# Attention followed by an MLP on one core: score matmuls of two key slots back to back, 112-wide query tiles, a six-bank tail and new pacing

## The chip, the cores and the metric

The kernel runs on one core of a Trainium2 chip. The metric is the device time of one execution in microseconds (us). Ratios below use runs in the fast state alone. Medians are of all runs of a kernel; a_single and a_fix_r2 each hold one slow run, which is said there. Each experiment ran on one chip together with runs of the kernel before. The changed kernel itself ran only in the first rounds, so a difference in us to it crosses rounds (the medians of the kernel before lay between 497.8 and 500.1 us in them); the ratios to the kernel before are the safer comparison.

AV stands for attention times V, the second product of the attention. The names of the engines are those of the profile: PE is TensorE's matmuls, PEld its weight loads, DVE is VectorE, ACT ScalarE, POOL GpSimd.

## The reference, cut to what matters

```python
# q, k, v: (8, 12, 448, 64) float32, g_q and g_k: (64,)
q_n, k_n = rmsnorm(q, g_q), rmsnorm(k, g_k)
scores = q_n @ k_n.transpose / sqrt(64)
attn   = softmax(scores)
x      = (attn @ v), heads put side by side      # (3584, 768)
h      = x @ w_in                                # (3584, 2048)
g      = h * clip(h + 3, 0, 6) / 6
out    = g @ w_out                               # (3584, 768) float32
```

There are 8 batches of 12 heads. The kernel takes two heads at a time, a pair: 48 pairs, six to a batch. When the six pairs of a batch are done, its MLP can begin.

## The kernel before

The kernel does not issue its operations in source order. It records each with a cost, a wanted time and the resources that it reads and writes. A small list scheduler, the plan, then orders them: each engine takes, of what it takes to be available, the operation with the earliest wanted time. So the order on every engine is fixed when the program is built, by a model of the hardware; at run time each engine works through its list, and semaphores make it wait where the model was too hopeful. PE writes its results to banks of PSUM; the first lines of the cut share these banks out. "Gate" in the cut is the last product of g, a VectorE operation.

```python
S_r = [psum.tile([128, 2, 512], FP32, name=f"S{i}") for i in range(2)]   # 2 tiles of 2 banks
X_ps = psum.tile([128, 2, 512], FP32, name="X")                          # 2 banks
M_r = [psum.tile([128, 512], FP32, name=f"M{i}") for i in range(2)]      # 2 banks

def score(P, t, want):            # one of four key slots of a pair, 112 keys
    # ... [cut]
    def f_s():
        for a in range(2):        # the two heads: rows 0-63 and 64-127 of the array
            r = slice(a * 64, a * 64 + 64)
            em(nc.tensor.matmul(out=ps[:, a, 0:S], lhsT=kT[r, t * TP:t * TP + 128], rhs=qT[r, :], ...))
    def f_e():
        em(nc.scalar.activation(out=eT[:, t], in_=ps[0:TP, :, 0:S], func=EXP, bias=0.0, scale=1.0))

C0 = [0, 128, 256, S - 128]       # four query tiles of 128, the last two overlap
def av(P, t, want):
    # ... [cut]
    for a in range(2):
        for i in range(NQT):
            em(nc.tensor.matmul(out=X_ps[:, a, i * E1:(i + 1) * E1],
                                lhsT=eT[:, t, a, C0[i]:C0[i] + 128], rhs=va[:, a, t, :], ...))

# MLP: 16 h groups of a batch (6 matmuls of 448 columns, relu on ACT, gate on DVE),
#      y groups (2 x 16 matmuls of 384 columns, copy on ACT); banks M0 and M1 in turn
em(nc.scalar.activation(out=ts[:], in_=ps[:, 0:S], func=RELU, bias=half_c[:], scale=1.0 / 6.0))
# ... [cut: loads, normalisation, transposes, output]

T0, DP0, DP = 8.0, 4.0, 8.5       # wanted times: a pair every 4 us, from the second batch on every 8.5 us
...
base = at(P + 1)                  # MLP work of a batch is spread from the start of the next batch on
span = at(P + NPAIR + 1) - base
```

The transposes of q and k go into the score tiles S0 and S1, in turn with the scores.

## Time and profile before

| kernel before | |
|---|---|
| time, median of the first 3 runs | 499.28 us (498.3 to 501.03) |
| PE busy | 461.8 us, 93% of the span |
| ACT, DVE, POOL busy | 59%, 47%, 43% |
| chain that ended last | PE 81% |
| score matmuls, busy | 72.5 us |

A timeline of the kernel before, PE only, shows what a score pair costs (columns: start, duration, instruction; the ends of matmuls overlap the next start):

```profile
200.12 0.36 PE L303 MATMUL S<-qT,kT 64*128 64x448 bf16 x2
200.42 1.47 PE L397 MATMUL M<-w_out_sb,gT 128*128 128x384 bf16 x8
201.73 0.39 PE L342 MATMUL X<-identity,xn 128*128 128x128 bf16 x4
```

Eight w_out matmuls take 1.31 us from their first start to the next instruction's, 163 ns each. The two score matmuls run side by side in the two halves of the array, but the next instruction starts 0.30 us after them, not the 0.19 us that 448 columns take elsewhere (a w_in matmul: 189 ns). And 0.1 us is lost on the way in. Over the whole trace a trip into half-array mode and back costs about 0.2 us, and there are 173 of them. That is the term that the change attacks.

### The profile page before, as it was taken

The page shows a single profiled execution, that of the slowest core. Times are in us where ns is not written, and L with a number is a line of the kernel's source. Part 1 is how long each engine was busy: PE and PEld are TensorE (multiplying, and loading weights), DVE is VectorE, ACT ScalarE, POOL GpSimd, SP SyncE. Part 2 cuts the span into 40 slices and gives each one's busy share as a digit, 9 for nine tenths or more (in the row PEclk, how much of TensorE's full clock was granted, in tenths as well). Part 3 has the DMA queues.
Part 4 walks back from the last instruction along what each step waited for, and adds up shares of the span by engine and source line. Part 5 has one row for each costly group of instructions (what it writes and reads, how often), then busy time and mean ns, then how long its engine had stood idle before and what let it go on. Part 6 is the DMA issues. An engine that isn't in the chain of part 4 may idle for free.

```text
span 497.3 us, 10192 instructions
## 1 busy us (share of the span) xinstructions
PE 461.8 (93%) x4160; PEld 264.9 (53%) x4160; DVE 234.5 (47%) x432; ACT 295.1 (59%) x485; POOL 213.6 (43%) x204
## 2 busy tenths in 40 slices
PE   1688999899998999899999999999999999989996
PEld 0355556456555555565555555555555555545563
DVE  4766576465864255545546254455434233322200
ACT  5566778767775367656666475666657456533311
POOL 4886594598963146536256063545223000000000
PEclk9999899999999999999999999999999999999999
DMA  7999984254422145333233243332110111111122
GB/s 207 254 245 265 243 190 127 75 161 140 136 74 89 34 125 144 96 97 98 87 110 92 70 125 92 101 97 85 55 32 2 33 34 34 34 32 30 34 59 69
DMA packets 44463, 50.99 MB, mean 103 GB/s; under 512 B 3456, under 2 KB 40832, under 8 KB 44416
## 3 DMA queue, kind: packets, MB, share of 16 engines
q1 hardware_dynamic: 39040, 44.05, 31.4%
q0 software_dynamic: 5376, 6.29, 7.2%
q8 instruction: 32, 0.52, 0.4%
q14 instruction: 15, 0.12, 0.1%
HBM read 45.61 MB, written 11.01 MB: 114 GB/s over the span
## 4 chain that ended last, share of the span: by engine, by line
PE 81%; DMA 7%; DVE 3%; ACT 3%; issue 2%; POOL 2%; SPq 1%; POOLq 0%; ACTq 0%; DVEq 0%
PE M L397 30%; PE M L364 26%; PE S L303 9%; PE X L320 9%; DMA qk<-in_k_dram 6%; PE S L283 3%; PE X L342 2%; ACT eT L308 2%; DMA qk<-in_q_dram 1%; DVE gT L375 1%; ACT ts L372 1%; POOL qks L253 1%; DVE xn L335 1%; SPq L201 1%; DVE ssq L227 0%
## 5 line engine op out<-in xcount | busy, mean ns | idle before, releaser
L308 ACT ACTIVATE eT<-S 112x896 bf16<-112x896 f32 x192 | 171.8, 916 | 61.4 <-PE S L303 59.9
L364 PE MATMUL M<-xT,w_in_sb 128*128 128x448 bf16 x768 | 171.0, 354 | 4.1 <-DVE gT L375 3.8
L397 PE MATMUL M<-w_out_sb,gT 128*128 128x384 bf16 x896 | 160.2, 326 | 0.5 <-DVE gT L375 0.5
L253 POOL TENSOR_TENSOR qks<-qk,rs 112x512 bf16<-112x512 f32 x87 | 91.8, 1076 | 118.4 <-PE S L283 86.8
L375 DVE SCALAR_TENSOR_TENSOR gT<-ts,M 128x448 bf16<-128x448 f32 x128 | 78.5, 618 | 105.3 <-ACT ts L372 104.6
L372 ACT ACTIVATE ts<-M,half_c 128x448 f32<-128x448 f32 x128 | 80.5, 636 | 59.5 <-PE M L364 57.3
L397 PEld LDWEIGHTS <-gT 128*128 128x128 bf16 x896 | 82.3, 98 | 60.3 <-issue 11.1
L364 PEld LDWEIGHTS <-w_in_sb 128*128 128x128 bf16 x768 | 67.1, 98 | 64.0 <-issue 17.7
L224 POOL TENSOR_TENSOR sq<-qk 112x1024 f32<-112x1024 f32 x45 | 84.8, 1894 | 9.9 <-DMA qk<-in_k_dram 4.0
L320 PEld LDWEIGHTS <-eT 112*128 112x128 bf16 x1536 | 64.3, 101 | 26.2 <-issue 7.0
L303 PE MATMUL S<-qT,kT 64*128 64x448 bf16 x384 | 72.5, 380 | 5.7 <-DVE kT L291 3.0
L320 PE MATMUL X<-va,eT 112*128 112x65 bf16 x1536 | 72.8, 199 | 1.9 <-ACT eT L308 1.2
L227 DVE TENSOR_REDUCE ssq<-sq 112x16 f32<-112x1024 f32 (+1 forms) x51 | 58.5, 1151 | 17.0 <-POOL sq L224 11.8
L406 ACT COPY y<-M 128x384 f32<-128x384 f32 x56 | 26.8, 478 | 63.7 <-PE M L397 63.7
L264 POOL CAST va<-vf 112x512 bf16<-112x512 f32 x48 | 29.7, 618 | 61.0 <-issue 26.6
L283 PE MATMUL S<-identity,qks 112*128 112x112 bf16 x384 | 32.4, 223 | 15.9 <-DVE qks L253 12.4
L283 PEld LDWEIGHTS <-qks 112*128 112x128 bf16 x384 | 24.8, 102 | 28.4 <-DVE qks L253 13.7
L303 PEld LDWEIGHTS <-kT 64*128 64x128 bf16 x384 | 19.0, 94 | 36.7 <-issue 27.9
L335 DVE TENSOR_TENSOR xn<-X,rd 128x512 bf16<-128x512 f32 x48 | 33.2, 692 | 1.7
L346 DVE COPY xT<-X 128x448 bf16<-128x448 bf16 x48 | 18.7, 389 | 31.1 <-PE X L342 30.8
L289 DVE COPY qT<-S 128x448 bf16<-128x448 bf16 x48 | 18.7, 389 | 28.2 <-PE S L283 17.3
L291 DVE TENSOR_SCALAR kT<-S,gp_t 128x448 bf16<-128x448 bf16 x48 | 21.4, 445 | 18.2 <-PE S L283 18.2
(23 smaller groups left out, 93.2 us busy)
## 6 DMA issues: line engine op xcount, KB each, us to landing
qk<-in_q_dram SPq DMA_DIRECT2D x48, 224.0 KB, 3.0
qk<-in_k_dram SPq DMA_DIRECT2D x48, 224.0 KB, 3.5
vf<-in_v_dram SPq DMA_DIRECT2D x48, 224.0 KB, 3.1
w_in_sb<-in_moe_w_in_dram POOLq DMA_DIRECT2D x4, 768.0 KB, 14.3
w_out_sb<-in_moe_w_out_dram POOLq DMA_DIRECT2D x4, 768.0 KB, 10.9
out_dram<-y SPq DMA_DIRECT2D x8, 336.0 KB, 2.8
out_dram<-y SPq DMA_DIRECT2D x8, 288.0 KB, 2.7
out_dram<-y SPq DMA_DIRECT2D x8, 240.0 KB, 2.7
```

The costliest lines, as they stand in the source:

```text
L224: em(nc.gpsimd.tensor_tensor(out=o, in0=x, in1=x, op=A_MULT))
L227: em(nc.vector.tensor_reduce(out=ssq[:, s].rearrange("p i n -> p (i n)"), in_=sq[:, s].rearrange("p i (n d) -> p (i n) d", d=D), axis=AX_X ...
L253: em((nc.vector if eng is DVE else nc.gpsimd).tensor_tensor(out=qks[:, i].rearrange("p t h d -> p h t d"), in0=qk[:, i].rearrange("p h (t ...
L283: em(nc.tensor.transpose(ps[:, t * TP:(t + 1) * TP], qks[:, i, t].rearrange("p h d -> p (h d)"), identity[0:TP, 0:TP]))
L303: em(nc.tensor.matmul(out=ps[:, a, 0:S], lhsT=kT[r, t * TP:t * TP + 128], rhs=qT[r, :], start=True, stop=True))
L308: em(nc.scalar.activation(out=eT[:, t], in_=ps[0:TP, :, 0:S], func=EXP, bias=0.0, scale=1.0))
L320: em(nc.tensor.matmul(out=X_ps[:, a, i * E1:(i + 1) * E1], lhsT=eT[:, t, a, C0[i]:C0[i] + 128], rhs=va[:, a, t, :], start=(t == 0 and i == ...
L335: em(nc.vector.tensor_tensor(out=xn[:].rearrange("p i a d -> p a i d"), in0=xv[:, :, :, 0:D], in1=rd[:].unsqueeze(3).to_broadcast([128, 2, ...
L364: em(nc.tensor.matmul(out=ps[:, 0:S], lhsT=w_in_sb[:, kt, f * 128:(f + 1) * 128], rhs=xT[:, kt, :], start=(kt == 0), stop=(kt == NKT - 1)))
L372: em(nc.scalar.activation(out=ts[:], in_=ps[:, 0:S], func=RELU, bias=half_c[:], scale=1.0 / 6.0))
L375: em(nc.vector.scalar_tensor_tensor(out=gT[:, f, e * S:(e + 1) * S], in0=ts[:], scalar=1.0, in1=ps[:, 0:S], op0=A_MIN, op1=A_MULT))
L397: em(nc.tensor.matmul(out=ps[:, 0:HALF], lhsT=gT[:, f, i * 128:(i + 1) * 128], rhs=w_out_sb[:, f, n * HALF:(n + 1) * HALF], start=(f == 0) ...
```

## The change

The intent: halve those trips, by issuing the score matmuls of two key slots in one run of four over all four banks of S; take 112 query rows to a tile, so that no row is computed twice; drop pointer biases on ScalarE; let the tail, where no attention is left, use six banks instead of two; and give each batch as much planned time as its own work needs. The diff, cut to its core:

```diff
-    eT_r = ring(NE, [TP, T, 2, S], BF16, "eT")
+    T_r = ring(NT, [128, S2 + PAD], BF16, "T")            # q and k transposed, in one tile
+    eT_r = ring(NE, [TP, T * S2 + PAD], BF16, "eT")       # PAD = 16 columns, once, after the last slot
...
+    for i, g in enumerate((g_q, g_k)):                     # for a path that is not taken (NPT = 48)
+        nc.gpsimd.dma_start(out=gb_t[:, i], in_=g...to_broadcast([TP, D]))
...
-                    out=rs[:, s], in_=ssq[:, s], func=LN, bias=eps_c[0:TP, :]))
+                em(nc.scalar.activation(out=rs[:, s], in_=ssq[:, s], func=LN, bias=D * 1e-6))
...
-    def score(P, t, want):
+    def score(P, ts, want):
+            for t, u in zip(ts, slots):                    # two key slots: four matmuls, S0 and S1
+                for a in range(2):
+                    em(nc.tensor.matmul(out=S_r[u][:, a, 0:S], lhsT=qkT[r, S + t * TP:S + t * TP + 128], ...))
...
-                        lhsT=eT[:, t, a, C0[i]:C0[i] + 128],
+                    c = t * S2 + a * S + i * TP
+                        lhsT=eT[:, c:c + 128],
...
+    banks = [M_r[0], M_r[1]] + [S_r[u][:, i] for u in range(2) for i in range(2)]
+        nb = 6 if b == B else 2                            # tail: six banks
...
-            em(nc.scalar.activation(out=ts[:], ..., func=RELU, bias=half_c[:], scale=1.0 / 6.0))
+            em(nc.scalar.activation(out=ts[:], ..., func=RELU, bias=0.5, scale=1.0 / 6.0))
...
+    start = [8.0, 33.0]
+    for b in range(1, B):
+        start.append(start[-1] + NFT * H_C + len(ys[b]) * Y_C + NPAIR * A_C)
...
+        two = [[0], [1], [2], [3]] if P < NPAIR else [[0, 1], [2, 3]]
...
+        w = start[b] + 2.0                                 # MLP of batch b-1: from 2 us after the start of batch b
```

The transposes of q and k of most pairs now go into one bank, the first of S0. The plan's cost constants were brought up to date as well.

## The prediction

> What bounds the kernel now. The page puts PE at 461.8 of 497.3 us (93%), ACT at 59%, DVE 47%, POOL 43%; the chain of waits that ended last is PE for 81%. By stages (busy time in windows) PE is busy 27 of the first 43 us, 48.7 of every 50 us from 100 to 400 us, and about 69 of the last 77. So the middle is PE time alone.
>
> Where PE time goes, from starts of successive matmuls in the trace: a w_out matmul takes 163 ns, a w_in matmul 189, an AV matmul 29 to 35, a q/k transpose 49. A score pair (two 64-row matmuls) starts 3 ns apart, but the next full-array matmul follows 292 ns later instead of 189, and the matmul before a pair takes about 96 ns extra (285 against 189, 258 against 163, 127 against 29). A trip into half-array mode and back thus costs about 0.2 us. The Trainium skill, "TensorEngine Tiling (Array Packing)", Key Properties, says a change of tiling mode drains TensorE; the trace agrees with these 0.2 us.
>
> What the change does.
> 1. Order of the built programs: 173 separate runs of score matmuls before, 100 after (90 of four matmuls); 4160 matmuls in both. 73 trips fewer x 0.2 us = about 14.6 us of PE time, on the critical path.
> 2. Query tiles of 112: 192 output transposes stream 112 columns instead of 128 (56 to about 49 ns): 1.3 us.
> 3. Immediate biases: relu (636 ns x128) and ln (308 ns x45) lose a pointer operand. The Trainium skill, "ScalarE: Activation LUTs", What ACT_TABLE_LOAD costs, gives about 93 ns for each; the trace fits (448 elements should leave about 545 ns). ACT loses about 16 us, but is idle 41%: little on the critical path.
> 4. Tail over six banks: from 440 to 470 us groups of 12 w_in matmuls (2.43 us) alternate with 0.25 to 0.3 us of PE waiting for the gate on DVE. That goes: about -2.7 us.
> 5. Start: transposes leave the score banks; first batch needs 17 instead of 20 score runs, at the cold rate (a pair 560 ns, not 360). About -2 us.
> 6. Given back: a run of four needs both score slots free, that is two exps (2 x 0.92 us) done, and the q/k transposes now sit in one of the same banks. At the change of batch the new order has three such runs with only 0.7 to 0.9 us of other PE work between them and no MLP work left; scheduled by hand with the durations above, PE stalls about 2.5 us there, five or six times, against about 1.3 us before (0.92 + 0.36 at 208 to 210 us). About +7 us.
>
> Sum: -14.6 -1.3 -2.7 -2 -2 (fewer small waits before 100 us) +7, about -15 us: 484 us, 3% faster.
>
> What would show it: score pairs in runs of four, the second pair starting about 190 ns after the first; score busy time down from 72.5 to about 58 us; relu mean about 543 ns; no gate waits on PE after 440 us; new waits of scores on exp and of scores on the k copy at batch changes, about 10 to 17 us in total; w_in and w_out means unchanged.
>
> What would make it wrong: much larger stalls of the four-runs on exp (then within 2%); a late gain broadcast (a new small DMA) holding up VectorE at the start; or new pacing that closes gaps I count as kept (then below 477).
>
> Predicted 484 us, 8 in 10 within 475 to 493; faster by over 2% 0.74, within 2% 0.24, slower 0.02.

## More of the kernel before

From the page of the kernel before: the first lines are busy time by engine and the busy tenths in 40 slices (PEclk is the granted TensorE clock), then the chain, then groups (busy us, mean ns of one, idle time of the engine just before them).

```profile
PE 461.8 (93%) x4160; PEld 264.9 (53%) x4160; DVE 234.5 (47%) x432; ACT 295.1 (59%) x485; POOL 213.6 (43%) x204
...
PE   1688999899998999899999999999999999989996
...
PEclk9999899999999999999999999999999999999999
...
PE 81%; DMA 7%; DVE 3%; ACT 3%; issue 2%; POOL 2%; SPq 1%; POOLq 0%; ACTq 0%; DVEq 0%
...
L372 ACT ACTIVATE ts<-M,half_c 128x448 f32<-128x448 f32 x128 | 80.5, 636 | 59.5 <-PE M L364 57.3
...
L320 PE MATMUL X<-va,eT 112*128 112x65 bf16 x1536 | 72.8, 199 | 1.9 <-ACT eT L308 1.2
L303 PE MATMUL S<-qT,kT 64*128 64x448 bf16 x384 | 72.5, 380 | 5.7 <-DVE kT L291 3.0
```

PE is the engine to look at: its row is 9 nearly throughout, and AV matmuls (L320) wait for almost nothing.

## The result

| | before | after |
|---|---|---|
| time, median (range), 4 runs each | 500.07 us (498.3 to 501.03) | 515.92 us (515.8 to 518.24) |
| PE busy | 461.8 us | 461.8 us |
| runs of score matmuls in the program | 173 | 100 |
| mean granted clock in the profile | 0.996 | 0.964 |

The ratio of after to before is 1.0332 (95% interval 1.0288 to 1.0376): 3.3% slower, where 3% faster was predicted. A ratio here is the mean time of one kernel's fast runs over that of the other's of the same rounds, so it is not quite the ratio of the medians quoted.

The page after, the same lines:

```profile
PE 461.8 (89%) x4160; PEld 261.0 (51%) x4160; DVE 236.8 (46%) x436; ACT 275.9 (53%) x485; POOL 213.7 (41%) x204
...
PE   2878997999989999899989999899998999978895
...
PEclk9988999899979999899988999889998999999999
...
PE 71%; ACT 14%; DVE 8%; issue 3%; POOL 2%; DMA 1%; POOLq 0%; DVEq 0%; ACTq 0%
...
L429 ACT ACTIVATE ts<-M 128x448 f32<-128x448 f32 x117 | 63.7, 544 | 59.9 <-PE M L421 59.3
...
L372 PE MATMUL X<-va,eT 112*128 112x65 bf16 x1536 | 81.4, 201 | 12.9 <-ACT eT L360 11.2
...
L351 PE MATMUL S<-T 64*128 64x448 bf16 x384 | 60.2, 386 | 9.8 <-DVE T L333 8.1
...
L451 PE MATMUL S<-w_out_sb,gT 128*128 128x384 bf16 x144 | 25.3, 326 | 4.6 <-ACT y L460 1.7
```

Score matmuls did get cheaper (72.5 to 60.2 us busy), and the relu fell to 544 ns. But PE's busy time as a whole did not fall, the AV matmuls now wait 12.9 us instead of 1.9, the clock row has dips, and ACT has 14% of the chain.

To see where, I cut the trace of every kernel into nine stages, each ending at the last output transpose of a batch; the ninth is the MLP tail. For each stage, "work" is the number of matmuls of each kind times its undisturbed spacing in these traces (163, 189, 49, 31 ns; 95 ns for a score matmul), "trips" is 0.2 us for each run of score matmuls, "idle" is PE's gaps, and "other" is the rest: matmuls that took longer than undisturbed, above all at a lower clock. "Half" is time at a clock of 0.5, of the recorded intervals. These are my sums over the records of the profile, in us:

```
before              duration  work  trips  idle  other   half
  stages 1-2            87.7  48.5    8.4  14.2   16.6    3.4
  stages 3-8           340.9 301.8   26.2   7.6    5.4    0.0
  stage 9 (tail)        57.2  53.4    0.0   2.6    1.2    0.0
  all                  485.7 403.7   34.6  24.3   23.1    3.4
after
  stages 1-2            90.5  51.8    5.8  17.5   15.5   10.2
  stages 3-8           351.5 298.6   14.2  18.2   20.4   27.3
  stage 9 (tail)        63.1  53.4    0.0   7.9    1.8    0.0
  all                  505.1 403.7   20.0  43.7   37.7   37.5
```

The work is the same, and the trips fell by 14.6 us (73 runs fewer at 0.2 us; the busy time of the score matmuls, measured by itself, fell by 12.3 us, and the second pair of a run starts 196 ns after the first). Against that stand 19.4 us more idle time and 14.6 us more of slow matmuls. The sum of the three, 19.4 us, agrees with the 19.2 us between the two spans (516.5 less 497.3). So there are two questions: where does the idle time come from, and why did the clock fall?

Two cautions about "half". The clock records begin at the first change (42.7 us before, 25.3 us after), so the figures of stages 1-2, and with them the mean clocks, can't be compared; score pairs take about 0.56 us, as at half clock, in both kernels before that. And a profile is one execution. In a run further down (a_tail4) PE's order is the same up to the tail, but stages 3-8 have 10.2 us of half clock instead of 27.3; and the four executions of the changed kernel show mean clocks from 0.964 to 0.987, worked out some 24 us of half clock apart (the profile's first stage has 6.8), with times within 2.4 us of each other. So the amounts of half clock, and part of "other", are those of the execution shown.

What PE waited for between 100 us and the last batch (line waiting, line waited for, total us, times, longest), first before, then after:

```profile
PE S L303 <- DVE kT L291: 3.0, 4, 0.9
PE M L364 <- DVE gT L375: 1.7, 2, 1.1
PE S L303 <- ACT eT L308: 1.0, 3, 0.4
...
```

```profile
PE X L372 <- ACT eT L360: 7.7, 26, 0.4
PE S L351 <- DVE T L333: 5.4, 9, 0.7
PE S L324 <- ACT eT L360: 1.9, 4, 0.5
...
```

And the PE timeline at one change of batch, before and after (brackets: idle time before it and what ended that):

```profile
207.72 0.36 PE L303 MATMUL S<-qT,kT 64*128 64x448 bf16 x2
208.99 0.36 PE L303 MATMUL S<-qT,kT 64*128 64x448 bf16 x2 [0.92 <-DVE kT L291]
209.29 0.42 PE L320 MATMUL X<-va,eT 112*128 112x65 bf16 x8
209.64 0.36 PE L303 MATMUL S<-qT,kT 64*128 64x448 bf16 x2
210.36 0.37 PE L303 MATMUL S<-qT,kT 64*128 64x448 bf16 x2 [0.36 <-ACT eT L308]
...
211.47 0.74 PE L364 MATMUL M<-xT,w_in_sb 128*128 128x448 bf16 x3
```

```profile
208.44 0.55 PE L351 MATMUL S<-T 64*128 64x448 bf16 x4 [0.71 <-DVE T L333]
208.93 0.63 PE L372 MATMUL X<-va,eT 112*128 112x65 bf16 x15
209.82 0.41 PE L372 MATMUL X<-va,eT 112*128 112x65 bf16 x8 [0.26 <-ACT eT L360]
210.62 0.20 PE L372 MATMUL X<-va,eT 112*128 112x65 bf16 x1 [0.39 <-ACT eT L360]
210.76 0.55 PE L351 MATMUL S<-T 64*128 64x448 bf16 x4
211.25 0.42 PE L372 MATMUL X<-va,eT 112*128 112x65 bf16 x8
212.13 0.55 PE L324 MATMUL S<-identity,qks 112*128 112x112 bf16 x8 [0.47 <-ACT eT L360]
212.69 0.37 PE L403 MATMUL X<-identity,xn 112*128 112x112 bf16 x4
213.60 0.93 PE L351 MATMUL S<-T 64*128 64x448 bf16 x4 [0.53 <-DVE T L333]
214.46 1.30 PE L421 MATMUL M<-xT,w_in_sb 128*128 128x448 bf16 x3
```

Three things are to be seen in the second timeline. No MLP matmul (L421, L451) stands between 208.4 and 214.4 us, so PE has nothing to fill its waits with. AV matmuls come as 15 and then one alone that waits for an exp; that one is the eighth of its group. And the first MLP matmuls after the stretch take 1.30 us for three, where before they take 0.74: the clock has fallen. Busy time in windows around these places, first before, then after (columns: PE, PEld, DVE, ACT, POOL busy with counts, then the clock, the DMA share and GB/s):

```profile
207.70:211.50 3.80, 2.48 (x25) 1.15 (x24) 1.98 (x5) 3.35 (x6) 3.50 (x4) 1.00 0.55 160
```

```profile
137.00:148.00 11.00, 9.54 (x112) 5.36 (x110) 6.02 (x12) 7.35 (x13) 6.50 (x6) 1.00 0.37 100
148.20:155.00 6.80, 6.36 (x41) 3.08 (x41) 2.57 (x6) 4.18 (x7) 4.54 (x4) 0.50 0.59 165
...
207.50:213.60 6.10, 3.73 (x58) 2.31 (x56) 3.88 (x9) 3.83 (x6) 4.54 (x5) 0.95 0.42 121
213.60:216.40 2.80, 2.80 (x17) 1.19 (x17) 0.26 (x2) 2.16 (x3) 2.80 (x3) 0.50 0.68 182
```

PE was busy 3.73 of 6.10 us in the stretch, 61%, and right after it the clock is 0.50 while PE is fully busy. The bill for the lull is paid by the dense MLP work that follows.

The Trainium skill, "TensorE: Matmul & The Clock Gate", Part 1, describes this gate: activity is judged in windows of about 3.4 us that run on their own, and the clock is half or full. The trace agrees on both: all half-clock intervals are 3.4 us long or a multiple of it, at 0.5. But the page's table lets the clock fall after an idle window (a passage on a second failure mode also names frequent micro-idles between groups of matmuls, without a number), and here PE was never idle for longer than 0.82 us between 80 and 430 us. I come back to that.

### The profile page after: what moved, and what is told of

The parts are those of the page before. It is cut to its first block, busy times and chain, and to the rows that moved or that the text cites. A ratio compares the mean times of both kernels' runs of the same rounds, so it can differ in the third digit from the quotient of the medians.

```text
span 516.5 us, 10221 instructions
## 1 busy us (share of the span) xinstructions
PE 461.8 (89%) x4160; PEld 261.0 (51%) x4160; DVE 236.8 (46%) x436; ACT 275.9 (53%) x485; POOL 213.7 (41%) x204
## 4 chain that ended last, share of the span: by engine, by line
PE 71%; ACT 14%; DVE 8%; issue 3%; POOL 2%; DMA 1%; POOLq 0%; DVEq 0%; ACTq 0%
PE M L451 22%; PE M L421 21%; ACT eT L360 10%; PE X L372 8%; PE S L351 7%; PE S L451 5%; PE S L324 3%; DVE gT L432 3%; PE S L421 2%; ACT ts L429 2%; DVE ssq L250 2%; DMA gb_t<-in_g_k_dram 1%; PE X L403 1%; POOL sq L247 1%; DVE T L331 1%
## 5 line engine op out<-in xcount | busy, mean ns | idle before, releaser
L421 PE MATMUL M<-xT,w_in_sb 128*128 128x448 bf16 x702 | 159.0, 361 | 1.2 <-DVE gT L432 1.2
L451 PE MATMUL M<-w_out_sb,gT 128*128 128x384 bf16 x752 | 138.3, 327 | 0.1
L451 PEld LDWEIGHTS <-gT 128*128 128x128 bf16 x896 | 82.8, 98 | 59.4 <-issue 11.2
L421 PEld LDWEIGHTS <-w_in_sb 128*128 128x128 bf16 x768 | 69.4, 99 | 68.9 <-issue 20.8
L429 ACT ACTIVATE ts<-M 128x448 f32<-128x448 f32 x117 | 63.7, 544 | 59.9 <-PE M L421 59.3
L372 PE MATMUL X<-va,eT 112*128 112x65 bf16 x1536 | 81.4, 201 | 12.9 <-ACT eT L360 11.2
L351 PE MATMUL S<-T 64*128 64x448 bf16 x384 | 60.2, 386 | 9.8 <-DVE T L333 8.1
L387 DVE TENSOR_TENSOR xn<-X,rd 112x512 bf16<-112x512 f32 x48 | 33.2, 691 | 1.7
L384 DVE RECIPROCAL rd<-X 112x8 f32<-112x8 f32 x48 | 9.9, 206 | 51.4 <-PE X L372 51.1
L351 PEld LDWEIGHTS <-T 64*128 64x128 bf16 x384 | 13.5, 95 | 33.4 <-issue 28.7
L451 PE MATMUL S<-w_out_sb,gT 128*128 128x384 bf16 x144 | 25.3, 326 | 4.6 <-ACT y L460 1.7
L331 DVE COPY T<-S 128x448 bf16<-128x448 bf16 x40 | 15.6, 390 | 27.7 <-PE S L324 26.9
```

The lines of the kernel that those rows point to most:

```text
L351: em(nc.tensor.matmul(out=S_r[u][:, a, 0:S], lhsT=qkT[r, S + t * TP:S + t * TP + 128], rhs=qkT[r, 0:S], start=True, stop=True))
L372: em(nc.tensor.matmul(out=X_ps[:, a, i * E1:(i + 1) * E1], lhsT=eT[:, c:c + 128], rhs=va[:, a, t, :], start=(t == 0 and i == 0), stop=(t = ...
L387: em(nc.vector.tensor_tensor(out=xn[:].rearrange("p i a d -> p a i d"), in0=xv[:, :, :, 0:D], in1=rd[:].unsqueeze(3).to_broadcast([TP, 2, ...
L421: em(nc.tensor.matmul(out=ps[:, 0:S], lhsT=w_in_sb[:, kt, f * 128:(f + 1) * 128], rhs=xT[:, kt, :], start=(kt == 0), stop=(kt == NKT - 1)))
L451: em(nc.tensor.matmul(out=ps[:, 0:HALF], lhsT=gT[:, f, i * 128:(i + 1) * 128], rhs=w_out_sb[:, f, n * HALF:(n + 1) * HALF], start=(f == 0) ...
```

## The experiments

Theory A: at a change of batch the new program has no MLP work left, and what makes the loss is that stretch: waits that nothing fills, then half clock. Rival B: the runs of four, each needing two finished exps, make the stalls wherever they stand, whatever the pacing. Two more suspects came out of the trace: the lone eighth AV matmul, and the tail.

### Round 1: one part at a time

**a_single**: the changed kernel with its runs of four undone.

```diff
-        two = [[0], [1], [2], [3]] if P < NPAIR else [[0, 1], [2, 3]]
+        two = [[0], [1], [2], [3]]
```

> The changed kernel with its score matmuls issued pair by pair again (171 runs of score matmuls instead of 100), everything else kept. Theory A (the new pacing uses up the MLP work before each batch change; in the stretch of attention work alone that follows PE idles and its clock is halved): the program order still has seven such stretches of 3.3 to 4.2 us of PE work, so the clock still falls to half at the batch changes, and about 71 more trips into half-array mode at 0.2 us are added: 515 to 530 us, no faster than the changed kernel. Theory B (the runs of four, which need two finished exps, make the stalls by themselves): the stalls and the half clock go, 495 to 505 us.

Measured: 508.8 us, with one slow run among the four (506.5 us without it), ratio to before 1.0181 (1.0098 to 1.0264). Both missed. By the fast runs it is 9 us better than the changed kernel, not worse (against A), and just above B's range, 7 us behind the kernel before. In the stages it has 34.6 us idle instead of 43.7, and two of the batch changes, not six, still led to half clock, 6.8 us each (against B, which had all of it go). So the runs of four are part of the stalls, and not the whole.

**a_off12**: runs of four kept, the MLP work of a batch held back.

```diff
-        w = start[b] + 2.0
+        w = start[b] + 12.0
```

> The changed kernel with the planned start of each batch's MLP work held back from 2 us to 12 us after the start of the next batch's attention, so that MLP work is left for the batch change; runs of four kept (100). In its program order the stretches without MLP work after the first two batches are gone (one of 2.7 us is left). Theory A: no half-clock intervals from about 100 to 400 us, PE waits on exp and on the k copy there fall from about 17 us to under 6 us, 482 to 492 us. Theory B: the waits on exp remain wherever two runs of four follow each other, above 503 us.

Measured: 500.11 us, ratio 1.0028 (0.9961 to 1.0094): 16 us better than the changed kernel with one number, but outside both ranges. No half clock between 50 us and the end, as A said; in stages 3 to 8 "other" fell from 20.4 to 9.6 us. But the waits on exp hardly fell: from 100 to 420 us PE's AV matmuls still waited 6.0 us for them, 24 times (7.7 us, 26 times, in the changed kernel); what went were the waits on the k copy (5.4 to 0.5 us). With MLP work around them these waits can hardly come from the stretch. That pointed to the eighth AV matmul.

**a_tail4**: four banks in the tail, one of each PSUM tile.

```diff
-    banks = [M_r[0], M_r[1]] + [S_r[u][:, i] for u in range(2) for i in range(2)]
+    banks = [M_r[0], M_r[1], S_r[0][:, 0], S_r[1][:, 0]]
-        nb = 6 if b == B else 2
+        nb = 4 if b == B else 2
```

The reason is in the built program of the changed kernel. A tail matmul into the second bank of S0 (offset 512) waits for an instruction that reads the first (offset 0); the lines are cut to tile and offset:

```
Matmult S0@512 <- xT1@1344, w_in   waits for  Activation ts0@0 <- S0@0
Matmult S1@512 <- w_out, gT1@7296  waits for  TensorScalarPtr gT1@7616 <- ts0@0, S1@0
```

> The changed kernel with the tail over four PSUM banks that lie in four different tiles, instead of six banks of which four lie in two tiles of two banks each. In the changed kernel's program a tail matmul into the second bank of such a tile waits for the read of the first bank. If that false wait is why the tail still stalls: PE's idle time after 440 us falls from 8.2 us to under 3 us and the run is 4 to 7 us shorter than the changed kernel, 509 to 512 us. If not (the stall is ScalarE and VectorE emptying the banks), it stays within 2 us of 516 us.

Measured: 502.88 us, ratio 1.0067 (1.0008 to 1.0126), 13 us better, where 4 to 7 were expected. PE's idle time in the tail went from 7.9 us to 0.0. The tail itself is 9.8 us shorter (63.1 to 53.3 us, and 53.4 is its work); the rest of the 13 us is fewer half-clock intervals elsewhere (23.9 instead of 37.5 us), which no part of this edit explains: PE's order is the same up to the tail, so it is a difference between executions. The tail after, and the same in this run:

```profile
476.61 2.43 PE L421 MATMUL S<-xT,w_in_sb 128*128 128x448 bf16 x12 [0.69 <-ACT ts L429]
479.73 0.73 PE L421 MATMUL S<-xT,w_in_sb 128*128 128x448 bf16 x3 [0.69 <-ACT ts L429]
```

```profile
463.16 2.43 PE L421 MATMUL M<-xT,w_in_sb 128*128 128x448 bf16 x12
465.43 2.43 PE L421 MATMUL S<-xT,w_in_sb 128*128 128x448 bf16 x12
```

The dependency tracking counts a tile of two banks as one thing here. Six banks in four tiles left more idle time (7.9 us) than the two banks in two tiles of the kernel before (2.6 us), and four banks in four tiles less than both.

**b_four**: the kernel before with runs of four alone.

```diff
-        for t in range(2):
-            score(P, t, w + t * step)
+        two = [[0], [1], [2], [3]] if P < NPAIR else [[0, 1], [2, 3]]
+        for n, ts in enumerate(two):
+            score(P, ts, w + ts[0] * step)
```

> The kernel before with only its score matmuls in runs of four (102 runs instead of 173); pacing, transposes and tail as before. Its own program order now has six stretches of 3.3 to 6.7 us of attention work without MLP work, where before has four. Theory A: the 14 us won by fewer trips are largely lost at these stretches, with half-clock intervals at batch changes, 492 to 508 us. Rival (the old pacing is harmless, only the new one hurts): 483 to 489 us with a clock of 1.0.

Measured: 510.02 us, ratio 1.0211 (1.0141 to 1.0281), just above the range of A and far from the rival's. So the old pacing is not harmless either. My reading is that with cheaper scores the plan runs its MLP work ahead of the attention; stretches like those of the changed kernel appear (17.4 us of idle time from 100 to 440 us, 20.5 us of half clock in all).

### Round 2: the eighth AV matmul, and the repairs together

With 112-wide query tiles the weight load of AV still takes 128 columns. For seven of the eight loads of a slot the last 16 are columns of the same slot. For the eighth they lie in the next slot, because the padding stands once, after the last slot. The results of these columns are never used, but the load reads them, so it waits for the next slot's exp. In the changed kernel's trace 40 of the AV matmuls that waited are eighth ones, with 11.0 us; before, all 9 that waited are first ones, with 1.9 us. In a_single, which has the same padding, 4 eighth ones waited, 1.1 us: it takes the runs of four to make this wait cost much. (The Trainium skill, "TensorE: Matmul & The Clock Gate", Weight-path perf modes, gives a reason to keep to 128 columns: only a load of 128 weights takes the fast path. No run here tests that.)

**a_pad**: padding of its own for each slot.

```diff
-    eT_r = ring(NE, [TP, T * S2 + PAD], BF16, "eT")
+    eT_r = ring(NE, [TP, T * (S2 + PAD)], BF16, "eT")
-                    c = t * S2 + a * S + i * TP
+                    c = t * (S2 + PAD) + a * S + i * TP
```

> The changed kernel with one edit: each key slot of the exp tile gets its own 16 padding columns. In the changed kernel the eighth AV matmul of a slot loads 128 columns of which the last 16 belong to the next slot, so it waits for the next slot's exp; the trace shows 40 such waits, 11.0 us. If that is a cause: no waits at the eighth AV matmul, PE idle time 9 to 11 us lower, fewer half-clock intervals, 498 to 508 us. If those waits only hide another wait behind them (the next run of scores needs the same exp anyway): within 3 us of the changed kernel's 516 us.

Measured: 500.71 us, ratio 1.0074 (1.0033 to 1.0115): 15 us better than the changed kernel (13 by the ratios). The place of the timeline above in this run; all sixteen AV matmuls of two slots now come together, and no lone one follows:

```profile
203.77 0.66 PE L372 MATMUL X<-va,eT 112*128 112x65 bf16 x16
204.65 0.42 PE L372 MATMUL X<-va,eT 112*128 112x65 bf16 x8 [0.23 <-ACT eT L360]
```

AV's waits for exp fell from 11.2 to 2.2 us. Idle time fell by 7.1 us (43.7 to 36.6), less than expected because other waits grew (transposes for the scaled q and k from 12.5 to 14.7 us), and "other" fell by 10.8 us, as half clock went from 37.5 to 10.2 us. So the gain is larger than the idle time that went. My reading is that these short waits pulled lulls below what keeps the clock up; how much of the gain is that stays open, since half clock differs between executions.

**a_fix**: the three edits together (a_pad, a_tail4, a_off12).

> The changed kernel with the three repairs together: own padding for each slot, tail over four banks in four tiles, MLP work held back 12 us instead of 2 us; runs of four kept. If the repairs act on separate stalls their gains add: idle after the first score about 44 us down to about 18 us, one half-clock interval at most after 50 us, 478 to 488 us. If they overlap (one stall behind another), 490 to 496 us.

Measured: 476.86 us, ratio 0.9611 (0.9544 to 0.9677): 3.9% faster than before and just below the range of the first expectation. The single edits gave 15, 13 and 16 us, together they give 39 (by the ratios 13, 13 and 15, together 36), so they act on nearly separate stalls. From its page:

```profile
PE 443.4 (93%) x4160; PEld 253.5 (53%) x4160; DVE 235.1 (49%) x436; ACT 271.8 (57%) x485; POOL 213.9 (45%) x204
...
PEclk9998999999999999999999999999999999999999
```

PE's busy time is now 18.4 us below that of before, and its waits for exp and for the k copy between 100 and 410 us are down to 0.7 us. Stages 3 to 8 have 4.5 us idle (7.6 before) and 3.6 us "other" (5.4 before).

**a_fix_s12**: besides, the second batch pair by pair too (`P < 2 * NPAIR` in place of `P < NPAIR`).

> The three repairs and, besides, the score matmuls of the first two batches (not only the first) pair by pair. In the second batch little MLP work exists yet, and its program order then has no stretch of more than 2.5 us without it. If the runs of four are what stalls the second batch: its stage gets 2 to 4 us shorter than with the three repairs alone, for 1.6 us of extra trips; if the second batch is held up by input or by VectorE, no gain.

Measured: 476.14 us, ratio 0.9577 (0.9537 to 0.9616). In the profile the second stage is 1.6 us shorter (46.2 against 47.8), a small gain, where 2 to 4 us were expected. That profiled run, 482.06 us, had a slow first stage; the median is level with a_fix, within the spread of either.

**b_tail4_imm**: the kernel before with only immediate biases and the four-tile tail.

> The kernel before with only the immediate biases and a tail over four banks in four tiles. The relu should fall from 636 to 544 ns as in the changed kernel. The tail's 2.6 us of idle time goes; the rest of ScalarE's saving is off the critical path: 2 to 4 us faster than before, 495 to 497.5 us. If ScalarE had been on the critical path in the middle, more than 6 us faster.

Measured: 492.35 us, ratio 0.9881 (0.9834 to 0.9929), 3 us better than expected. The tail's idle time went from 2.6 us to 0.0, as expected. The profile has another 3.6 us less idle time in the other stages, mostly at the start; the two edits were not tried one by one, so which of them it was stays open.

### Round 3: what the runs of four are worth, and the clock

**a_fix_single**: a_fix with score matmuls pair by pair.

> The repaired kernel (own padding, four tail banks in four tiles, MLP work held back) with its score matmuls pair by pair (175 runs instead of 100). If the 0.2 us per trip into half-array mode is real and on the critical path once the stalls are gone: 75 x 0.2 = 15 us slower than the repaired kernel, 488 to 494 us. If the runs of four were worth nothing: 475 to 480 us.

Measured: 483.31 us, ratio 0.9698 (0.965 to 0.9745). Between the two expectations: the runs of four are worth 6.4 us by the medians, which come from different rounds (by the ratios 4 us against a_fix and 6 against a_fix_r2 below), not 15. The stages show why. Trips cost 35.0 us instead of 20.0, but idle time is 14.5 us instead of 20.7, and "other" 16.8 instead of 19.3. Single pairs stall less; of the 15 us that the runs of four save, about 6 come back as waits and 2.5 as slower matmuls even in the repaired kernel.

**a_fill**: the changed kernel with throw-away matmuls in the lulls. Results stay right, since the scores overwrite them.

```diff
+        fills = 2 if P >= 11 and (P % NPAIR == 0 or (P % NPAIR == NPAIR - 1 and ts[0] == 2)) else 0
         def f_s():
+            for _ in range(fills):
+                em(nc.tensor.matmul(out=S_r[slots[0]][:, 0, 0:S], lhsT=identity[:], rhs=qkT[:, 0:S], ...))
```

> The changed kernel with two full-array matmuls of 448 columns (results thrown away, 0.38 us) before each of the three runs of four that stand in the stretch without MLP work at a batch change. Theory: in such stretches the clock is halved because TensorE does too little dense work; the fills leave all waits in place but the half-clock intervals between 90 and 400 us (about 31 us of them in the changed kernel's profile) go or shrink to under 10 us; the time falls by up to 10 us although 20 matmuls and more are added, 505 to 514 us. If the clock falls for another reason, the intervals stay and the time rises by 3 to 8 us.

Measured: 518.43 us, ratio 1.0388 (1.0337 to 1.0439). The clock did what the theory said: no half-clock interval is left between 51 us and the end, where the changed kernel has six with 30.7 us; all waits are still there (47.1 us idle). The window after the first of those changes in this run has a clock of 1.00, where the changed kernel had 0.50:

```profile
152.00:159.00 7.00, 5.54 (x70) 3.02 (x71) 1.95 (x5) 4.76 (x9) 4.61 (x5) 1.00 0.49 143
```

The time did not fall, a miss. In stages 3 to 8 "other" is 9 us less (11 instead of 20), but the fills are 6 us of added work and idle time grew by 1 us, which leaves a gain of 2 us; and in this execution the first batch, where no fill stands, took 4 us longer. So too little PE work in these stretches does cause the half clock, and the remedy is to have real work there. The comparison also sizes it: with no half clock, "other" in these stages is still 11 us, against 5.4 in the kernel before. That rest is not the clock, and was not taken apart.

**a_warm**: a_fix with 40 matmuls at the start and two fills before each score pair of the first batch.

> The repaired kernel with 40 matmuls of 128 columns at the very start and two full-array matmuls of 448 columns (results overwritten) before each score pair of the first batch. [...]Theory (attention matmuls alone, with 64 rows or 65 columns, do not keep the clock up): the score pairs of the first batch fall from 560 ns to about 360 ns each and the first batch ends 2 to 8 us earlier, 469 to 476 us. If the clock stays halved: the fills add about 10 us, 484 to 490 us.

Measured: 476.76 us, ratio 0.956 (0.9512 to 0.9608), level with a_fix. From 18 us on the score pairs take 0.36 us and no longer 0.56, so with the fills the clock is up from there to the end of the first batch. It is not so that attention alone can't raise it: the changed kernel's profile has full clock from 25.3 to 28.7 and from 32.1 to 42.4 us, before its first MLP matmul at 46.3 us. But the first batch ended at 47.2 us against 48.0: again the fills ate the gain.

**a_fix_nogb**: a_fix without the gain broadcast that nothing reads.

> The repaired kernel without the broadcast load of the gains and the VectorE instruction that multiplies them, which nothing reads here. VectorE waits for that load about 12 us into the changed kernel, before the second batch of sums. If it is on the critical path at the start: 0.5 to 2 us faster than the repaired kernel; if not, the same within 1 us.

Measured: 473.36 us, ratio 0.948 (0.9417 to 0.9543), 3.5 us below a_fix, which had run in other rounds, and more than either expectation; so it was run again.

### Round 4: what was still open

**a_pad_t4**: a_pad and a_tail4 without the held-back MLP.

> The changed kernel with own padding for each slot and the four-tile tail, but its own pacing of the MLP work. If the stretches without MLP work at the batch changes are a cause of their own: the stages from the third to the seventh keep 2 to 3 us of PE idle time each, and the run is 8 to 14 us slower than the repaired kernel of the same rounds, 484 to 492 us. If the padding waits were all of it: within 3 us of the repaired kernel.

Measured: 490.44 us, ratio 0.9836 (0.9786 to 0.9885), 13 us behind a_fix of the same rounds. Stages 3 to 7 keep 2.0 to 3.3 us of idle time each, where a_fix has 0.6 to 1.1, so the stretches without MLP work are a cause of their own.

**a_fix_r2** and **a_nogb_r2**: a_fix and a_fix_nogb again, in the same rounds.

> The repaired kernel again, for comparison in the same rounds: 475 to 479 us.

> The repaired kernel without the unused gain broadcast again, in the same rounds as the repaired kernel. If the broadcast delays VectorE on the critical path: 1 to 4 us faster than it; if the earlier 3.5 us were the difference of two chips or rounds: the same within 1 us.

Measured: 477.41 and 476.62 us, both with ratio 0.9582. In the profiles the first stage is 3.4 us shorter without the broadcast (38.7 against 42.1), but the timed runs overlap (473.8 to 479.52 us, and 476.61 to 477.97 without a slow run of 484.04), and the means of the fast runs are 0.5 us apart (476.6 and 477.1). What the broadcast costs is not settled; 0 to 3 us.

**best_s12**: a_nogb_r2 with the second batch pair by pair.

> The repaired kernel without the gain broadcast and with the first two batches pair by pair: as fast as the repaired kernel without the broadcast, within 2 us, 471 to 476 us; the second batch's stage 1 to 3 us shorter, the trips there 1.6 us dearer.

Measured: 474.61 us (473.59 to 476.04), ratio 0.9533 (0.9495 to 0.9571). The second stage is 2 us shorter than in a_nogb_r2, as expected. This is the fastest version in its rounds, 4.7% faster than before, but its lead over a_nogb_r2 is within the spread of the runs.

### When the clock fell

Over the traces of all 18 kernels I laid the 3.4 us grid of the clock records and took PE's busy share, as the profile gives it, in each window at full clock. There are 47 falls away from the end of a run. Of these 46 followed a window with a busy share between 0.35 and 0.70; one, in a_warm, followed a window without a matmul. No window above 0.70 was followed by a fall, and every one below 0.56 was. Windows between 0.56 and 0.70 went either way, so the share alone does not decide: in the changed kernel a window of 0.57 in the tail, among w_in and w_out matmuls, kept the clock, and one of 0.69 at a batch change lost it. The kernel before has one at 0.68 without a fall and one at 0.66, at 46 us, with a fall; its lull of the timeline above falls into a window of 0.73. So in these profiles the kernel before lived just above the edge, and the changed kernel fell below it six times in a row.

## Why the prediction was wrong

The predicted time was 484 us, with 475 to 493 as its range; the time is 515.9 us.

1. Trips: right in size as PE time. 14.6 us were predicted for 73 trips, and the busy time of score matmuls fell by 12.3 us (58 us predicted, 60.2 measured). But "on the critical path" holds only in part: a_fix against a_fix_single shows 4 to 6 us net for 75 trips.
2. Transposes of 112 columns: right, 49 ns each. But the prediction saw only this side of the 112-wide tiles. It missed that the eighth AV load reaches into the next slot: 11.0 us of waits in the trace, and 15 us when repaired (a_pad). This could have been read from the diff: 128 columns from the last tile start of a slot end 16 columns past it.
3. Immediate biases: right. The relu fell from 636 to 544 ns, 92 ns for one pointer operand, which agrees with the 93 ns of the Trainium skill, "ScalarE: Activation LUTs", What ACT_TABLE_LOAD costs.
4. Tail: wrong in sign. Predicted: 2.7 us of idle time gone. Measured: 5.3 us more (2.6 to 7.9), because two banks of one tile wait for each other in the built program. The idea was right once the banks lie in different tiles (a_tail4, b_tail4_imm: 0.0 us idle).
5. Start: mis-sized. About 2 us and 2 us of small waits were counted as gained in the first 100 us. In the first two stages trips, idle and other together went from 39.2 to 38.8 us, a gain of 0.4 us. The trips alone, which item 1 counts already, gave 2.6 of it, so idle and other grew by 2.2 us.
6. Given back: this is the step that failed most. The place was right (batch changes, no MLP work left, runs of four too close together), and "+7 us" was counted. Measured in stages 3 to 8: 10.6 us more idle time, of which the eighth AV matmul, which I had not seen, is a large part (its waits there are 8.5 us); and 15.0 us more of slow matmuls, which the prediction did not contain at all. About 9 of these 15 us are half clock (a_fill removes them); the rest stays open. The prediction treated a stall as costing its own length. Here a stall also slowed the dense work after it.

With the terms as measured: trips -14.6, idle +19.4, other +14.6 us, together +19.4 us. The list of what could go wrong named "much larger stalls of the four-runs on exp", with "then within 2%" as the worst case; a second-order loss by the clock was on no list. Not tried one by one: the transposes in one bank of S0 and the new cost constants of the plan; a_fix keeps both, so the loss does not need them undone.

## What to carry to other kernels

Making PE work cheaper can lose time in a scheduled kernel: filler work runs out earlier, the lull that appears pulls the clock down, and the next dense stretch pays; so check the busy share of the poorest few microseconds, not only the average, and keep filler work back for the places that need it. When a tile is repacked, check which columns each load really touches and which waits the built program got: garbage columns and two banks of one tile both bought waits here that no result needed. And when a change bundles several ideas, undo and repair them one by one: the idea of the runs of four was sound, and with three small repairs around it the kernel is 3.9% faster than before instead of 3.3% slower.

## What the Trainium skill lacked or had wrong

- "TensorE: Matmul & The Clock Gate", Part 1 and the table at its end: the page lets the clock fall after an idle window and warns of idle gaps of about 3 us; its passage on a second failure mode names frequent micro-idles, but gives no size. Here, between 80 and 430 us of the changed kernel, it fell after windows in which PE was busy 51 to 69% by the profile, with no gap above 0.82 us; over all traces no window above 70% led to a fall. Filler matmuls in the same lulls removed all six falls (a_fill).
- The same page lets one busy window raise the clock. In the kernel before, score pairs take 0.56 us instead of 0.36 until 42.7 us, although PE's busy share is 1.00 in the window from 32.5 to 35.9 us; in the changed kernel a window of 1.00 (18.5 to 21.9 us) did not raise it, and the next one, also 1.00, did. Part 4 of the page says that transposes do not count as busy in the same way; no run here tests whether that is why.
- "TensorEngine Tiling (Array Packing)", Key Properties, says that a change of tiling mode drains TensorE, without a number. Here: about 96 ns on the way in and 93 to 103 ns on the way out, 0.2 us for each trip of 64-row matmuls among 128-row ones.
- "TensorE: Matmul & The Clock Gate", Part 1, says that profiles hold the transitions of the clock, but not what follows from it: the records begin at the first change (42.7 us in the kernel before), so the granted clock reads 1.0 before that, while the durations of matmuls show half speed.
- No page has it: a PSUM tile of two banks was tracked as one thing by the built program, so matmuls into one bank waited for readers of the other: 7.9 us of idle time in the tail with six banks in four tiles, 0.0 with four banks in four tiles (a_tail4).
